# Half a phi moved ahead of the first x copy, the fourth numerators moved into the middle of out step 9, and two output copies swapped between engines: an attention and feed-forward kernel on one core

## The chip, the cores and the metric

The kernel runs on one core of a Trainium2 chip. The metric is the device time of one execution, in microseconds (us). The span of the profile runs from the program's first instruction to its last, and is some 2 us shorter than that time (324.5 against 326.26 us in the traced run of the kernel before). Names of engines: PE is the matmul engine, PEld its weight loads, DVE the vector engine, ACT the scalar engine, POOL the GpSimd engine, SP the engine whose queue issues most DMAs. L254 means line 254 of the kernel. Lines from 682 on carry a higher number in the changed kernel (L692 becomes L693), because a line was added before them.

## The reference

Batch 8, 8 heads, 576 tokens, head size 64; the result is a 4608 x 512 matrix.

```python
def phi(x, c, s):
    r = np.maximum(x, 0.0)
    return np.concatenate([r * c, r * s], axis=-1)   # cosine half, sine half
q_p, k_p = phi(q, cos_w, sin_w), phi(k, cos_w, sin_w)
kv  = einsum('bhsf,bhsd->bhfd', k_p, v);  z = k_p.sum over s
num = einsum('bhsf,bhfd->bhsd', q_p, kv)
den = einsum('bhsf,bhf->bhs', q_p, z)[..., None] + 1e-06
x   = (num / den), heads side by side: 4608 x 512
xn  = x / sqrt(mean(x * x) + 1e-6) * rms_g
out = (silu(xn @ w_gate) * (xn @ w_val)) @ w_out
```

## The kernel before

It works on one batch after another, and places every instruction by hand: each engine executes its own instructions in the order in which the source emits them. While PE runs the feed-forward part (FFN) of one batch, the other engines prepare the next. The change touches the opening (first x tiles of batch 0) and the end of block 0 (out steps, while batch 1 is prepared). "Numerators" are the matmuls of `nd_pe` (L414); an "x tile" is 128 tokens of x. Names that begin with ps are banks, the buffers that PE writes and that the other engines copy from. A "releaser" is the instruction whose end lets a waiting instruction start.

```python
def q_phi(eng, b, c, part):            # for batch 0 a q tile has two halves
    ...
        for i in range(2 if c < 4 else 1):
            j = 2 * c + i
            phi(eng, qp_tiles[(b, c)][:, 4*i : 4*i+4, o], raw[("q", 0)][...], f(5 + j))
...
# opening
    filler(7, psV[1][:, :])
    q_tr_pe(0, 2, psO[0][:, :])        # PE: transposes of q tile 2
    x_scale(0, 0)                      # DVE: x tile 0 scaled
    # x tile 0: PE transposes, half copied by ACT, half by DVE ("the first x copy")
    q_phi(A, 0, 3, 1)                  # ACT: sine half of q tile 3
    q_tr_evac(A, 0, 2, psO[0][:, :])   # ACT: copy of q tile 2's transposes
    x_norm(0, 1)                       # DVE: x tile 1 normalized
    q_phi(V, 0, 3, 0)                  # DVE: cosine half of q tile 3, two instructions
    open_ffn(0, (0, 1), 0, 128)        # PE: first FFN matmuls
    x_tr_pe(0, 1, psV[1][:, :])
    x_tr_evac(V, 0, 1, psV[1][:, :])
    q_tr_pe(0, 3, psO[1][:, :])        # PE: transposes of q tile 3
    nd_pe(0, 2, psA)                   # PE: numerators of x tile 2
    ...
# out steps of block 0: four banks, one per tile of 128 tokens
    for n in range(NNT - 2):
        ...
        if n == 9:
            x_norm(1, 1); tr1(0, psV[0][:, :])
        if n in nd_at:                 # numerators of batch 1, tile 3 at n == 9
            nd_pe(1, j, psA); nd_post(1, j, psA); x_sq(1, j)
        for j in range(4):
            out_mm(0, j, n, banks0[j])
    x_norm(1, 2)
    tr1(1, psV[1][:, :])               # PE transposes, ACT copies
    ...                                # n = 10, 11; copies of banks 2 (DVE) and 3 (ACT)
    gval_mm(1, 0, 0, (0, 256))         # PE: first matmuls of block 1
    tr1(2, psA[:, 0, :])
    out_store(V, 0, 1, banks0[1])
    x_norm(1, 3)
    out_store(A, 0, 0, banks0[0])
    gval_mm(1, 1, 1, (0, 256), ((psG, wg),))
    x_tr_pe(1, 3, psC[1][:, :]); x_tr_evac(V, 1, 3, psC[1][:, :])
```

`banks0` is psC0, psC1, psG0, psG1.

Of the kernel before, what the change touches and what calls it, by code (L numbers as in the profile page):

```python
# [26 lines left out]
def kernel(  # L27
# [39 lines left out]
    V, A, G = nc.vector, nc.scalar, nc.gpsimd  # L67
# [179 lines left out]
    def view4(t, j):  # L247
        return t[:, :, :].rearrange("p h (j d) -> p h j d", d=D)[:, :, j, :]

    def phi(eng, out_ap, in_ap, scale):  # L250
        if eng is nc.scalar:
            nc.scalar.activation(out=out_ap, in_=in_ap, func=AF.Relu, scale=scale)  # L252
        else:
            eng.tensor_scalar(  # L254
                out=out_ap, in0=in_ap, scalar1=scale, scalar2=0.0, op0=ALU.mult, op1=ALU.max
            )
# [24 lines left out]
            src = flat[:, 2048:2304].rearrange("p (i d) -> p i d", d=D)  # L281
        phi(eng, kp_of(b)[:, 8 * c : min(8 * c + 8, 36), o], src, f(c))

    def q_phi(eng, b, c, part):
        o = slice(0, D) if part == 0 else slice(D, F)
        f = cos_of if part == 0 else sin_of
        if (b, c) not in qp_tiles:
            qp_tiles[(b, c)] = four.tile(
                [P, H if c < 4 else 4, F], BF16, name="qp", tag="qp" if c < 4 else "qpt"
            )  # L290
        if b == 0:
            for i in range(2 if c < 4 else 1):
                j = 2 * c + i
                f = cos_of if part == 0 else sin_of
                phi(
                    eng, qp_tiles[(b, c)][:, 4 * i : 4 * i + 4, o],
                    raw[("q", 0)][:, :, j * D : (j + 1) * D], f(5 + j),
                )
            return
        src = view4(raw[("q", b)], c) if c < 4 else raw[("qt", b)][:, :, :]  # L300
        phi(eng, qp_tiles[(b, c)][:, :, o], src, f(c))
# [15 lines left out]
    def q_tr_pe(b, c, bank):  # L317
        t = qp_tiles[(b, c)]
        dst = bank.bitcast(BF16).rearrange("p (h s) -> p h s", s=P)
        for h in range(H if c < 4 else 4):  # L320
            nc.tensor.transpose(dst[:, h, :], t[:, h, :], ident[:, :])  # L321

    def q_tr_evac(eng, b, c, bank, heads=(0, 8)):
        h0, h1 = heads if c < 4 else (0, 4)
        if b == 0:
            src = bank.bitcast(BF16).rearrange("p (i h s) -> p h i s", i=2, h=H)
            copy(
                eng, q_dst(b, c)[:, h0:h1, :].rearrange("p h (i s) -> p h i s", i=2),
                src[:, h0:h1, :, :],
            )  # L330
            return
        dst = bank.bitcast(BF16).rearrange("p (h s) -> p h s", s=P)
        copy(eng, q_dst(b, c)[:, h0:h1, :], dst[:, h0:h1, :])

    def copy(eng, o, i):
        if eng is nc.scalar:
            nc.scalar.copy(out=o, in_=i)  # L337
        else:
            eng.tensor_copy(out=o, in_=i)  # L339
# [53 lines left out]
    def kvz_pe(b, pst):  # L393
        kvz_mm(b, [pst[:, c, :] for c in range(2)])
# [7 lines left out]
    def kvz_evac(eng, b, pst, c):  # L402
        kvz_copy(eng, b, c, pst[:, c, :])
# [94 lines left out]
    def x_scale(b, j):  # L498
        xn = four.tile([P, DM], BF16, name="xn", tag="xn")
        nc.vector.tensor_scalar(  # L500
            out=xn[:, :], in0=xg[:, :], scalar1=rs_of[(b, j)][:, :], scalar2=None, op0=ALU.mult
        )
        xn_of[(b, j)] = xn

    def x_norm(b, j):
        xn = four.tile([P, DM], BF16, name="xn", tag="xn")
        nc.vector.scalar_tensor_tensor(  # L507
            out=xn[:, :], in0=x_of[(b, j)][:, 0:DM], scalar=rs_of[(b, j)][:, :], in1=gb[:, :],
            op0=ALU.mult, op1=ALU.mult,
        )  # L510
        xn_of[(b, j)] = xn
# [16 lines left out]
    def x_tr_pe(b, j, bank, part=(0, NDT)):  # L528
        xn = xn_of[(b, j)]
        dst = bank.bitcast(BF16).rearrange("p (t s) -> p t s", s=P)  # L530
        for t in range(*part):
            nc.tensor.transpose(dst[:, t, :], xn[:, t * P : (t + 1) * P], ident[:, :])

    def x_tr_evac(eng, b, j, bank, part=(0, 4)):
        dst = bank.bitcast(BF16).rearrange("p (t s) -> p t s", s=P)
        copy(eng, x_dst(b, j)[:, part[0] : part[1], :], dst[:, part[0] : part[1], :])
# [5 lines left out]
    def gval_mm(blk, n, bank, cols=(0, TB), parts=((psG, wg), (psV, wv))):  # L542
        x = xnT[blk]
        for pst, w in parts:
            for t in range(NDT):
                nc.tensor.matmul(  # L546
                    pst[bank][:, cols[0] : cols[1]],
                    lhsT=w[:, t, n * P : (n + 1) * P],
                    rhs=x[:, t, cols[0] : cols[1]],
                    start=(t == 0), stop=(t == NDT - 1),  # L550
                )
# [13 lines left out]
    def out_mm(blk, j, n, bank):  # L565
        nc.tensor.matmul(  # L566
            bank, lhsT=hTs[blk][:, n, j * P : (j + 1) * P], rhs=wo[:, n, :],
            start=(n == 0), stop=(n == NNT - 1),
        )

    def out_store(eng, blk, j, bank):
        osb = four.tile([P, DM], FP32, name="osb", tag="osb")
        copy(eng, osb[:, :], bank)
        rows0 = out[0:S, :].rearrange("(p j) m -> j p m", j=NJ)
        if blk == 0:
            for i in range(2):
                nc.sync.dma_start(
                    out=rows0[2 * j + i, :, :], in_=osb[64 * i : 64 * i + 64, :]
                )
        elif blk < 8:  # L580
            rows = out[blk * S : blk * S + 512, :].rearrange("(p j) m -> p j m", j=4)
            nc.sync.dma_start(out=rows[:, j, :], in_=osb[:, :])
        else:
            for i in range(2):
                r0 = (2 * j + i) * S + 512
                nc.sync.dma_start(
                    out=rows0[8, :, :] if i + j == 0 else out[r0 : r0 + 64, :],
                    in_=osb[64 * i : 64 * i + 64, :],
                )
# [89 lines left out]
    filler(7, psV[1][:, :])  # L679
    q_tr_pe(0, 2, psO[0][:, :])  # L680
    x_scale(0, 0)

    def open_ffn(pair, steps, c0, c1, first=0, parts=(0, 1)):

        x = xnT[0]
        for i, n in enumerate(steps):
            for a in parts:
                w = (wg, wv)[a]
                bank = pairs[pair][a]
                lo = 256 * (first + i) + c0 % 256  # L690
                for t in range(NDT):
                    nc.tensor.matmul(  # L692
                        bank[:, lo : lo + c1 - c0],  # L693
                        lhsT=w[:, t, n * P : (n + 1) * P], rhs=x[:, t, c0:c1],
                        start=(t == 0), stop=(t == NDT - 1),
                    )
# [14 lines left out]
    for half, (eng, bank) in enumerate(((A, psG[1]), (V, psV[1]))):  # L711
        part = (2 * half, 2 * half + 2)
# [2 lines left out]
    q_phi(A, 0, 3, 1)  # L715
    q_tr_evac(A, 0, 2, psO[0][:, :])
    x_norm(0, 1)
    q_phi(V, 0, 3, 0)
    open_ffn(0, (0, 1), 0, 128)
    x_tr_pe(0, 1, psV[1][:, :])  # L720
    x_tr_evac(V, 0, 1, psV[1][:, :])
# [76 lines left out]
    for nb in range(2, B):  # L798
        b = nb - 1
# [30 lines left out]
        for j in range(4):  # L830
            n = nds[j]
# [12 lines left out]
    for nb in range(3, B):  # L844

        b = nb - 2
        for i, which in enumerate(("k", "v", "q")):
# [5 lines left out]
            for p in range(5):  # L853
                n = (0, None, 6)[i] + p if b == 1 else 5 * i + p
# [26 lines left out]
    banks0 = [psC[0][:, :], psC[1][:, :], psG[0][:, :], psG[1][:, :]]  # L881

    def tr1(j, bank):
        x_tr_pe(1, j, bank)
        x_tr_evac(A, 1, j, bank)
# [3 lines left out]
    for n in range(NNT - 2):  # L889
        if n == 3:  # L890
            kvz_pe(1, psA)
            kvz_evac(A, 1, psA, 0)
            kvz_evac(V, 1, psA, 1)
        if 1 <= n <= 4:
            c = n - 1
            q_tr_pe(1, c, qbank[c])
            q_tr_evac(V if c < 2 else A, 1, c, qbank[c])
        if n == 0:
            for c in (1, 2, 3):
                q_phi(V, 1, c, 0)  # L900
                q_phi(A, 1, c, 1)
        if n == 1:
            v_cast(A, 1, *LOW)
            v_cast(V, 1, *HIGH)
        if n == 3:
            d = load_q_tail(1)
            tc.add_manual_dep(d.ins, wo_dmas[1].ins.name, SYNC_DEP, reason="after wo")
            load_kv("k", 2)
            load_q(2)
            load_q_tail(2)  # L910
            load_kv("v", 2)
        if n == 7:
            x_norm(1, 0)
        if n == 9:
            x_norm(1, 1)
            tr1(0, psV[0][:, :])
        if n in nd_at:
            j = nd_at[n]
            nd_pe(1, j, psA)
            nd_post(1, j, psA)  # L920
            x_sq(1, j)
        for j in range(4):
            out_mm(0, j, n, banks0[j])
    x_norm(1, 2)
    tr1(1, psV[1][:, :])
# [5 lines left out]
    for j in (0, 1):  # L931
        for n in (NNT - 2, NNT - 1):
            out_mm(0, j, n, banks0[j])
    gval_mm(1, 0, 0, (0, 256))
    tr1(2, psA[:, 0, :])
    out_store(V, 0, 1, banks0[1])
    x_norm(1, 3)
    out_store(A, 0, 0, banks0[0])
    gval_mm(1, 1, 1, (0, 256), ((psG, wg),))
    x_tr_pe(1, 3, psC[1][:, :])  # L940
    x_tr_evac(V, 1, 3, psC[1][:, :])
# [72 lines left out]
```

## Time and profile before

| | before |
|---|---|
| time, median of 6 runs | 326.46 us (326.31 to 326.73) |
| span of the profile | 324.5 us |
| PE busy | 316.2 us, 97% |
| DVE, ACT busy | 57%, 54% |

The page cuts the span into 40 slices of 8.1 us and gives each engine's busy share in tenths:

```profile
PE   8999999999999999999999999999999999999995
DVE  6875768787656765578267745772577133203410
ACT  6974865965665556645555466455644333223321
```

PE is full from the second slice on. DVE and ACT have room on average, but one of them or both are at 7 to 9 in slices 2, 3, 7 and 8, where the change acts. There an engine with a mean of 57% can hold PE up for a few tenths of a microsecond, and the change aims at such places. The prediction below shows their lines.

```profile
54.91 0.56 ACT L337 COPY xnT<-psV 128x512 bf16<-128x512 bf16 x1
55.58 0.60 PE L546 MATMUL psG<-xnT,wg 128*128 128x256 bf16 x4
```

The first is ACT's copy of x tile 1's transposes. It ends at 55.48, and PE's psG matmul at 55.58 reads what it wrote. That matmul starts 0.22 us after the one in front of it, as those before it do, so in this kernel the copy doesn't hold it up yet.

### The profile page before, as it was taken

The page shows a single profiled execution, that of the slowest core. Times are in us where ns is not written, and L with a number is a line of the kernel's source. Part 1 is how long each engine was busy: PE and PEld are TensorE (multiplying, and loading weights), DVE is VectorE, ACT ScalarE, POOL GpSimd, SP SyncE. Part 2 cuts the span into 40 slices and gives each one's busy share as a digit, 9 for nine tenths or more (in the row PEclk, how much of TensorE's full clock was granted, in tenths as well). Part 3 has the DMA queues.
Part 4 walks back from the last instruction along what each step waited for, and adds up shares of the span by engine and source line. Part 5 has one row for each costly group of instructions (what it writes and reads, how often), then busy time and mean ns, then how long its engine had stood idle before and what let it go on. Part 6 is the DMA issues. An engine that isn't in the chain of part 4 may idle for free.

```text
span 324.5 us, 6131 instructions
## 1 busy us (share of the span) xinstructions
PE 316.2 (97%) x2249; PEld 162.4 (50%) x2284; DVE 184.3 (57%) x398; ACT 173.8 (54%) x351; POOL 39.3 (12%) x85
## 2 busy tenths in 40 slices
PE   8999999999999999999999999999999999999995
PEld 3588465555445444554454445444544444444443
DVE  6875768787656765578267745772577133203410
ACT  6974865965665556645555466455644333223321
POOL 4660202001111110012001120120011000000000
PEclk9999999999999999999999999999999999999999
DMA  7999999898799775977597679856611400020014
GB/s 271 281 196 253 309 205 339 243 165 189 164 248 273 190 205 153 237 163 195 165 214 206 155 219 210 194 158 215 128 40 33 131 32 0 25 106 0 1 33 100
DMA packets 89377, 53.90 MB, mean 166 GB/s; under 512 B 56321, under 2 KB 81921, under 8 KB 89346
## 3 DMA queue, kind: packets, MB, share of 16 engines
q1 hardware_dynamic: 82304, 48.65, 57.4%
q0 software_dynamic: 6880, 4.72, 10.0%
q8 instruction: 18, 0.29, 0.4%
q10 hardware_dynamic: 162, 0.13, 0.2%
q14 instruction: 13, 0.11, 0.1%
HBM read 37.75 MB, written 9.44 MB: 145 GB/s over the span
## 4 chain that ended last, share of the span: by engine, by line
PE 93%; DVE 2%; ACT 2%; issue 1%; POOL 0%; DVEq 0%
PE psC L566 26%; PE psV L546 26%; PE psG L546 26%; PE psA L414 2%; PE psO L593 2%; PE psA L370 2%; PE psG L566 2%; PE psO L692 1%; PE psG L692 1%; PE psV L692 1%; PE psV L321 1%; ACT kpm L252 1%; PE psA L386 1%; ACT sg L555 0%; PE psA L422 0%
## 5 line engine op out<-in xcount | busy, mean ns | idle before, releaser
L561 DVE TENSOR_TENSOR hT<-psV,sg 128x512 bf16<-128x512 f32 x102 | 70.3, 689 | 96.0 <-PE psV L546 71.2
L555 ACT ACTIVATE sg<-psG 128x512 f32<-128x512 f32 x102 | 60.6, 594 | 64.5 <-PE psG L546 63.2
L546 PE MATMUL psV<-xnT,wv 128*128 128x512 bf16 (+1 forms) x365 | 92.1, 375 | 0.4
L546 PE MATMUL psG<-xnT,wg 128*128 128x512 bf16 (+1 forms) x352 | 90.9, 375 | 0.7
L566 PE MATMUL psC<-wo,hT 128*128 128x512 bf16 x382 | 88.2, 380 | 0.7
L546 PEld LDWEIGHTS <-wv 128*128 128x128 bf16 x416 | 40.6, 98 | 47.4
L566 PEld LDWEIGHTS <-hT 128*128 128x128 bf16 x420 | 40.2, 98 | 46.7
L546 PEld LDWEIGHTS <-wg 128*128 128x128 bf16 x416 | 38.5, 98 | 40.8 <-DVE xnT L339 0.4
L485 POOL TENSOR_TENSOR rs<-ms,mhalf 128x1 f32<-128x1 f32 x36 | 19.8, 549 | 187.6 <-ACT scr L480 187.6
L337 ACT COPY osb<-psC 128x512 f32<-128x512 f32 (+1 forms) x33 | 19.1, 579 | 43.1 <-PE psC L566 42.4
L507 DVE SCALAR_TENSOR_TENSOR xn<-xt,rs,gb 128x512 bf16<-128x512 f32 x35 | 26.5, 757 | 16.4 <-POOL rs L485 16.3
L480 ACT ACTIVATE scr<-xt 128x513 bf16<-128x513 f32 x36 | 22.9, 635 | 23.7 <-DVE xt L469 23.6
L252 ACT ACTIVATE kpm<-rk,tab 128x256 bf16<-128x256 f32 (+2 forms) x58 | 28.2, 545 | 1.5 <-DMA rk<-in_k_dram 1.5
L469 DVE TENSOR_TENSOR xt<-psA,rec 128x512 f32<-128x512 f32 x35 | 24.2, 691 | 1.2
L252 ACT ACTIVATE qp<-rq,tab 128x512 bf16<-128x512 f32 (+1 forms) x37 | 23.7, 661 | 0.0
L254 DVE TENSOR_SCALAR kpm<-rk,tab 128x128 bf16<-128x128 f32 (+2 forms) x64 | 20.5, 377 | 2.1 <-DMA rk<-in_k_dram 2.1
L254 DVE TENSOR_SCALAR qp<-rq,tab 128x512 bf16<-128x512 f32 (+1 forms) x37 | 16.0, 452 | 0.0
L414 PEld LDWEIGHTS <-qpT 128*128 128x128 bf16 x248 | 11.7, 98 | 6.7 <-issue 0.3
L414 PE MATMUL psA<-kvzs,qpT 128*128 128x65 bf16 x248 | 12.8, 194 | 0.3
L546 PE MATMUL psG<-xnt_tail,wg 128*128 128x512 bf16 x48 | 12.3, 379 | 0.1
L546 PE MATMUL psV<-xnt_tail,wv 128*128 128x512 bf16 x47 | 12.1, 379 | 0.0
L339 DVE CAST vvm<-rv 128x1024 bf16<-128x1024 f32 (+4 forms) x16 | 10.4, 674 | 0.0
(99 smaller groups left out, 183.8 us busy)
## 6 DMA issues: line engine op xcount, KB each, us to landing
out_dram<-osb SPq DMA_DIRECT2D x28, 256.0 KB, 2.5
rk<-in_k_dram SPq DMA_DIRECT2D x20, 256.0 KB, 3.2
rq<-in_q_dram SPq DMA_DIRECT2D x20, 256.0 KB, 3.1
rv<-in_v_dram SPq DMA_DIRECT2D x16, 256.0 KB, 3.2
rq<-in_q_dram SPq DMA_DIRECT2D x2, 1024.0 KB, 9.2
out_dram<-osb SPq DMA_DIRECT2D x14, 128.0 KB, 3.2
rv<-in_v_dram SPq DMA_DIRECT2D x3, 576.0 KB, 8.4
wo<-in_moe_w_out_dram POOLq DMA_DIRECT2D x4, 384.0 KB, 7.1
```

The source lines that it names most:

```text
L252: nc.scalar.activation(out=out_ap, in_=in_ap, func=AF.Relu, scale=scale)
L254: eng.tensor_scalar(out=out_ap, in0=in_ap, scalar1=scale, scalar2=0.0, op0=ALU.mult, op1=ALU.max)
L337: nc.scalar.copy(out=o, in_=i)
L414: nc.tensor.matmul(o[:, g, i, :], lhsT=qpT[(b, 0)][:, h, j * P : (j + 1) * P], rhs=kvz_of(b, h), start=True, stop=True,)
L469: nc.vector.tensor_tensor(out=xt[:, 0:DM].rearrange("p (b h d) -> p b h d", b=2, d=D), in0=o[:, :, :, 0:D], in1=rec[:, :, :].unsqueeze(3). ...
L480: nc.scalar.activation(out=scr[:, :], in_=xt[:, 0 : DM + 1], func=AF.Square, scale=1.0 / math.sqrt(DM), accum_out=ms[:, :],)
L485: nc.gpsimd.tensor_tensor(out=rs[:, :], in0=ms[:, :], in1=mhalf[:, :], op=ALU.pow)
L507: nc.vector.scalar_tensor_tensor(out=xn[:, :], in0=x_of[(b, j)][:, 0:DM], scalar=rs_of[(b, j)][:, :], in1=gb[:, :], op0=ALU.mult, op1=ALU. ...
L546: nc.tensor.matmul(pst[bank][:, cols[0] : cols[1]], lhsT=w[:, t, n * P : (n + 1) * P], rhs=x[:, t, cols[0] : cols[1]], start=(t == 0), sto ...
L555: nc.scalar.activation(out=sg[:, :], in_=psG[bank][:, :], func=AF.Silu)
L561: nc.vector.tensor_tensor(out=hTs[blk][:, n, :], in0=psV[bank][:, :], in1=sg[:, :], op=ALU.mult)
L566: nc.tensor.matmul(bank, lhsT=hTs[blk][:, n, j * P : (j + 1) * P], rhs=wo[:, n, :], start=(n == 0), stop=(n == NNT - 1),)
```

## The change

Its intent: let DVE do half of the late phi in an idle spell, give PE two output matmuls to do where it waited for a bank, and give DVE's copy of psC1 to ACT, so that the last normalization comes sooner.

```diff
-    def q_phi(eng, b, c, part):
+    def q_phi(eng, b, c, part, subs=(0, 1)):
...
-            for i in range(2 if c < 4 else 1):
+            for i in subs if c < 4 else (0,):
...
     x_scale(0, 0)
+    q_phi(V, 0, 3, 0, (0,))
...
-    q_phi(V, 0, 3, 0)
+    q_phi(V, 0, 3, 0, (1,))
...
             tr1(0, psV[0][:, :])
+        for j in range(2) if n == 9 else ():
+            out_mm(0, j, n, banks0[j])
         if n in nd_at:
...
-        for j in range(4):
+        for j in range(2 if n == 9 else 0, 4):
             out_mm(0, j, n, banks0[j])
...
+    out_store(A, 0, 1, banks0[1])
     tr1(2, psA[:, 0, :])
-    out_store(V, 0, 1, banks0[1])
     x_norm(1, 3)
-    out_store(A, 0, 0, banks0[0])
+    out_store(V, 0, 0, banks0[0])
```

## The prediction

> **What bounds the kernel now.** I read the page first: shares of busy time, then the chain that ended last.
>
> ```profile
> PE 316.2 (97%) x2249; PEld 162.4 (50%) x2284; DVE 184.3 (57%) x398; ACT 173.8 (54%) x351; POOL 39.3 (12%) x85
> PE 93%; DVE 2%; ACT 2%; issue 1%; POOL 0%; DVEq 0%
> ```
>
> PE is busy for 97% of the span, and the chain of work that ended last runs through it for 93%. The change removes no PE instruction, so only holes in PE's stream can be won, and those hide in the 324.5 - 316.2 = 8.3 us outside its busy time. So I went to the timeline at the places that the diff touches, about 15 to 20 us and 51 to 58 us (columns: start, us, engine, line, operation, count, idle time before).
>
> First place, the transposes of q tile 3 (L321) around the first x tiles:
>
> ```profile
> 15.97 0.49 DVE L500 TENSOR_SCALAR xn<-sg,rs 128x512 bf16<-128x512 f32 x1
> 16.95 0.29 DVE L339 COPY xnT<-psV 128x256 bf16<-128x256 bf16 x1 [0.49 <-PE psV L532]
> 17.36 0.75 DVE L507 SCALAR_TENSOR_TENSOR xn<-xt,rs,gb 128x512 bf16<-128x512 f32 x1
> 17.91 1.00 ACT L337 COPY qpT<-psO 128x1024 bf16<-128x1024 bf16 x1
> 18.03 0.89 DVE L254 TENSOR_SCALAR qp<-rq,tab 128x256 bf16<-128x256 f32 x2
> 18.49 0.24 PEld L321 LDWEIGHTS <-qp 128*128 128x128 bf16 x4
> 19.07 0.38 PE L321 MATMUL psO<-ident,qp 128*128 128x128 bf16 x4 [0.16 <-DVE qp L254]
> 19.29 0.41 PE L414 MATMUL psA<-kvzs,qpT 128*128 128x65 bf16 x8
> ```
>
> DVE sits idle for 0.49 us before the first x copy at 16.95. Later, two phi instructions (L254) occupy it from 18.03 to 18.92, and the last four q transposes begin only at 19.07, right behind them. A finer window shows the two phis as 0.34 us and 0.63 us, the long one beginning at 18.29.
>
> Second place, out step 9:
>
> ```profile
> 52.39 0.74 DVE L507 SCALAR_TENSOR_TENSOR xn<-xt,rs,gb 128x512 bf16<-128x512 f32 x1
> 52.52 0.40 PE L414 MATMUL psA<-kvzs,qpT 128*128 128x65 bf16 x8
> 53.05 0.16 DVE L465 TENSOR_SCALAR rec<-psA 128x8 f32<-128x8 f32 x1
> 54.09 0.74 DVE L507 SCALAR_TENSOR_TENSOR xn<-xt,rs,gb 128x512 bf16<-128x512 f32 x1
> 54.74 0.68 DVE L339 COPY osb<-psG 128x512 f32<-128x512 f32 x1
> 55.48 0.41 PEld L546 LDWEIGHTS <-wg 128*128 128x128 bf16 x4 [0.24 <-DVE osb L339]
> ```
>
> PE has issued the four transposes of x tile 0 from 52.00 on (four at 0.055, so to 52.22) and then waits to 52.52 for psA, which DVE reads to 52.47: a hole of 0.30 us. But DVE works back to back from 51.34 to 55.42, and PE's weight load at 55.48 waits for that very DVE copy of psG.
>
> Third place, the block's two last copies:
>
> ```profile
> 55.78 0.69 DVE L339 COPY osb<-psC 128x512 f32<-128x512 f32 x1 [0.35 <-PE psC L566]
> 56.38 0.74 DVE L507 SCALAR_TENSOR_TENSOR xn<-xt,rs,gb 128x512 bf16<-128x512 f32 x1
> 57.18 0.23 PEld L532 LDWEIGHTS <-xn 128*128 128x128 bf16 x4 [0.19 <-DVE xn L507]
> 57.62 0.42 DVE L339 COPY xnT<-psC 128x512 bf16<-128x512 bf16 x1 [0.49 <-PE psC L532]
> 58.10 0.33 PEld L546 LDWEIGHTS <-wg 128*128 128x128 bf16 x4 [0.36 <-DVE xnT L339]
> ```
>
> The normalization of x tile 3 stands behind an output copy; PE waits for it at 57.18, and again at 58.10 for the copy of its transpose.
>
> **What the Trainium skill says.** (1) "VectorE: DVE Perf Modes", section "Mode 2×_2P": a single-source instruction on SBUF operands can stream one tensor through both read ports, two results per cycle even in fp32. The trace agrees: phi takes 0.34 us for 256 elements and 0.47 for 512, so 0.13 us per 256 more. (2) "SBUF — State Buffer", section "SBUF: two separate sides": such an instruction and GpSimd exclude each other by a lock on a shared port pair. It fits that the 0.63 us phi lies beside weight DMA issues of POOL (18.05 to 18.80); that this is the cause the trace doesn't prove. (3) "Perfetto Trace Analysis", section "Tensor Engine Instruction (MATMUL, LD_WEIGHTS)": matmul ends are modelled, so I count holes from start to start.
>
> **The change part by part.** The order of instructions built from both kernels shows the same work everywhere, only moved.
>
> *Part 1, half a phi ahead of the first x copy.* The scaling of x at 15.97 lets DVE go on at about 16.4. A phi of 0.34 ends at about 16.75, before the copy can start at 16.95 (POOL is idle from 15.94 to 16.77, so I expect no stretching). The normalization at 17.36 waits for POOL's result (16.77 + 0.55), so it stays. The remaining phi takes the place of the quick one, 18.03 to 18.37. PE: x transposes from 18.17 to 18.39; first q half at once (it needs no late phi now), 18.39 instead of 18.52; second half at 18.61 instead of 19.07; all eight issued by 18.83. That would win 19.29 - 18.83 = 0.46. But the numerators (L414) need the copy of q tile 2 by ACT, 17.91 + 1.00 = 18.91, and with a handover of 0.06 (57.12 to 57.18 in the third place) they begin at about 18.98. Part 1 wins 19.29 - 18.98 = **0.31 us**. The copy of x tile 1 moves to about 18.62 to 19.02, in time.
>
> Does a later wait eat it? The timeline has PE nearly dense from 19.3 to 43.9; its waits there go to instructions which PE itself releases. Landings, from the DMA view (issue plus time to landing) against first use: third wv slice 13.93 + 8.5 = 22.4 against 23.56; fifth wg slice 18.78 + 11.9 = 30.7 against about 35; q of batch 1 30.84 + 7.3 = 38.1 against 40.2; v of batch 1 40.9 against 42.6; second wo slice 43.6 against 45.6. The smallest slack is 1.1 us, so 0.31 passes through.
>
> *Part 2, two output matmuls between the transposes and the fourth numerators.* They take 2 x 0.216 = 0.43 us and fill the hole of 0.30, so numerators begin at 52.65 instead of 52.52 and PE arrives 0.30 earlier at the end of the out steps. But DVE's post-processing of these numerators, at 53.05 before, now starts at 52.65 + 0.41 + 0.04 = 53.10. DVE's row (normalization, copy of psG) slides by 0.05 and ends at about 55.47; PE can load at 55.53 and its matmul begins at about 55.55 instead of 55.58. Part 2 alone wins **0.03 us**: the hole moves from 52.2 to before 55.5.
>
> *Part 3, the swap.* ACT takes the psC copy after its own at 55.38 (ends about 56.0), so to about 56.6. DVE goes from the psG copy to normalization 3, which must wait for POOL's factor (55.09 + 0.55 = 55.64, plus 0.05), and ends at about 56.5 instead of 57.12. PE then reaches its transposes without a wait: 55.55 + 0.43 + 0.44 + 0.22 + 0.43 = 57.07 instead of 57.19; psC is free by then. DVE is free for the copy of the transpose, so the hole before 58.10 keeps its length and moves with it, to 57.98. Parts 2 and 3 together win **0.12 us**. Up to 67.7 the chain is ACT and DVE work released by PE at 59.6, with k, q and v of batch 2 long landed (v at 49.72 + 9.9 = 59.6, used at 65.2); from there on it is PE again.
>
> Sum: 0.31 + 0.12 = 0.43 us, so 326.41 - 0.43 = **325.98 us**.
>
> **Rivals.** (a) *The hole of step 9 is won whole.* It would add some 0.27, so 325.7. For: 0.30 us of PE idleness does vanish. Against: DVE's unbroken row to 55.42 and the wait at 55.48. (b) *Part 1 costs where it should win:* the early phi is stretched like the 0.63 us one, ends at 17.03 and delays the x copy by 0.08, and the first FFN matmul with it. Its second pair of weights has about 0.1 us of slack, so even then little is lost; if POOL stretched the second phi as well, transposes would end near 19.1 and part 1 would win 0.2. Time 326.1. (c) *The opening's gain dies at a transfer:* 326.3. The landings speak against it. (d) *ACT becomes the bound in part 3:* with two output copies in a row it would free psC late. I count 56.6 against a need at 57.07; a miss of 0.3 would leave 326.2.
>
> **Range and chances.** The central sum is 0.43; rivals lie between 325.7 and 326.3, and runs of the kernel before differ by 0.25 among themselves. So 325.6 to 326.45. Over 2% would be 6.5 us, fifteen times the sum: 0.005 on either side.
>
> **What would show it.** Right: a 0.34 us phi inside DVE's idle time before 16.95; q transposes without a wait inside; numerators at about 18.98 released by ACT's copy, not by DVE; no hole near 52.2 (less 0.31 for the shift), but one of about 0.25 before the psG matmul at 55.2; no wait for normalization before the last transposes; span about 324.05. Wrong: the first FFN matmul later than 17.3; the shift at 30 us smaller than 0.25; a psG matmul 0.3 us earlier than I have it; a wait for ACT before the last transposes.

## The result, and the profile after

| | before | changed |
|---|---|---|
| time, median of 6 runs | 326.46 us (326.31 to 326.73) | 326.05 us (325.86 to 326.24) |
| span of the profile | 324.5 us | 324.1 us |

The ratio is 0.9987, with a 95% interval of 0.9974 to 0.9999. Ratios here are the mean time of one kernel's fast runs over that of the other's of the same rounds, so not quite the ratio of the medians quoted. The page of the changed kernel:

```profile
PE 317.8 (98%) x2284; PEld 162.2 (50%) x2284; DVE 184.7 (57%) x398; ACT 173.9 (54%) x351; POOL 39.1 (12%) x85
PE 90%; DVE 5%; ACT 2%; DMA 1%; issue 1%; DVEq 0%; ACTq 0%
```

PE's busy time seems to have gone up by 1.6 us. It has not: the trace before holds 2249 matmuls and this one 2284, for the same number of weight loads. Thirty-five records were missing before. So the 8.3 us outside PE's busy time, from which the prediction sets out, are too many: 6.3 us by the complete trace. This is why the rest of this document goes by starts, not by busy time.

**First place**, timeline of the changed kernel:

```profile
15.90 0.49 DVE L500 TENSOR_SCALAR xn<-sg,rs 128x512 bf16<-128x512 f32 x1
16.30 0.35 DVE L254 TENSOR_SCALAR qp<-rq,tab 128x256 bf16<-128x256 f32 x1
16.88 0.29 DVE L339 COPY xnT<-psV 128x256 bf16<-128x256 bf16 x1 [0.23 <-PE psV L532]
17.84 1.00 ACT L337 COPY qpT<-psO 128x1024 bf16<-128x1024 bf16 x1
17.95 0.35 DVE L254 TENSOR_SCALAR qp<-rq,tab 128x256 bf16<-128x256 f32 x1
18.33 0.61 PE L321 MATMUL psO<-ident,qp 128*128 128x128 bf16 x8
18.90 0.42 PE L414 MATMUL psA<-kvzs,qpT 128*128 128x65 bf16 x8
```

The early phi lies in what was DVE's idle time. The late one takes 0.35 us, the eight q transposes run in one piece, and the numerators come right after the end of ACT's copy (17.84 + 1.00 = 18.84).

**Second and third place:**

```profile
52.28 0.41 PE L414 MATMUL psA<-kvzs,qpT 128*128 128x65 bf16 x8
52.72 0.17 DVE L465 TENSOR_SCALAR rec<-psA 128x8 f32<-128x8 f32 x1
54.43 0.68 DVE L339 COPY osb<-psG 128x512 f32<-128x512 f32 x1
54.60 0.57 ACT L337 COPY xnT<-psV 128x512 bf16<-128x512 bf16 x1
55.16 0.36 PEld L546 LDWEIGHTS <-wg 128*128 128x128 bf16 x4 [0.59 <-DVE osb L339]
55.21 0.60 PE L546 MATMUL psG<-xnT,wg 128*128 128x256 bf16 x4
55.35 0.75 DVE L507 SCALAR_TENSOR_TENSOR xn<-xt,rs,gb 128x512 bf16<-128x512 f32 x1 [0.24 <-POOL rs L485]
56.74 0.39 PE L532 MATMUL psC<-ident,xn 128*128 128x128 bf16 x4
57.24 0.42 DVE L339 COPY xnT<-psC 128x512 bf16<-128x512 bf16 x1 [0.53 <-PE psC L532]
57.72 0.33 PEld L546 LDWEIGHTS <-wg 128*128 128x128 bf16 x4 [0.43 <-DVE xnT L339]
```

The hole before the numerators is gone, but PEld now idles 0.59 us before the psG load at 55.16, where it idled 0.24 before. The psG matmul waits for two copies that end almost together: DVE's at 55.11 (54.43 + 0.68) and ACT's at 55.17. The normalization no longer stands behind an output copy, and PE reaches the transposes at 56.74 without a wait. Yet the last weight load waits longer than before, 0.43 against 0.36.

**How shifts are measured from here on.** The opening's DMAs land a little differently in each run: DVE's first work on the loaded k starts between 4.35 and 4.81 us. In the fourteen traces the first FFN weight load behind the copies of x tile 0 starts between 17.19 and 17.64 us. In all of them it starts 1.29 us after DVE's scaling of x tile 0, which stands ahead of every change; so the early phi between the two doesn't delay it, and it can serve as the zero. PE executes the same list of weight loads in nearly the same order in all kernels (2284; e10_best splits some and has 2288), and none of their records is missing. So I take the start of the same weight load in two traces, after subtracting the difference at that first FFN load. A negative shift is earlier.

| shift of the changed kernel against before | us |
|---|---|
| numerators of x tile 2 (19 us) to out step 8 (50 us) | -0.31 |
| transposes of x tile 3 (57 us) | -0.38 |
| second tile pair of block 1 (59 us) | -0.31 |
| last weight load of the kernel | -0.32 |

So the changed kernel gains 0.31 us in the opening and nothing after it. Against the 0.40 us by which its span is shorter, 0.07 us is this trace's earlier first FFN load, which the change doesn't move.

### The profile page after: what moved, and what is told of

Same layout as the page of the kernel before. It is cut to its first block, busy times and chain, and to the rows that moved or that the text cites. A ratio compares the mean times of both kernels' runs of the same rounds, so it can differ in the third digit from the quotient of the medians.

```text
span 324.1 us, 6166 instructions
## 1 busy us (share of the span) xinstructions
PE 317.8 (98%) x2284; PEld 162.2 (50%) x2284; DVE 184.7 (57%) x398; ACT 173.9 (54%) x351; POOL 39.1 (12%) x85
## 4 chain that ended last, share of the span: by engine, by line
PE 90%; DVE 5%; ACT 2%; DMA 1%; issue 1%; DVEq 0%; ACTq 0%
PE psG L546 26%; PE psC L566 26%; PE psV L546 26%; PE psA L414 2%; PE psA L370 2%; DVE kpm L254 1%; PE psG L693 1%; PE psV L693 1%; DMA rk<-in_k_dram 1%; PE psO L693 1%; PE psG L566 1%; DVE vvm L339 1%; ACT kpm L252 1%; DVE qp L254 1%; PE psA L386 1%
## 5 line engine op out<-in xcount | busy, mean ns | idle before, releaser
L546 PE MATMUL psG<-xnT,wg 128*128 128x512 bf16 (+1 forms) x368 | 92.8, 374 | 0.3 <-DVE xnT L339 0.2
L566 PE MATMUL psC<-wo,hT 128*128 128x512 bf16 x396 | 89.4, 379 | 0.0
```

The lines of the kernel that those rows point to most:

```text
L546: nc.tensor.matmul(pst[bank][:, cols[0] : cols[1]], lhsT=w[:, t, n * P : (n + 1) * P], rhs=x[:, t, cols[0] : cols[1]], start=(t == 0), sto ...
L566: nc.tensor.matmul(bank, lhsT=hTs[blk][:, n, j * P : (j + 1) * P], rhs=wo[:, n, :], start=(n == 0), stop=(n == NNT - 1),)
```

## The experiments

Twelve kernels ran, on three chips; each gave the reference's result. "Shift" is against the kernel before, as above. Times are medians of the fast runs. e7_act_early, e8_dve_early and e12_both_phis_early ran once, so their state is unknown; they are used for their traces alone. e11_pool_quiet is told below.

| kernel | shift at 59 us | shift at the end | time, us | before, same chip |
|---|---|---|---|---|
| changed | -0.31 | -0.32 | 326.05 | 326.46 |
| e1_part1 | -0.31 | -0.31 | 326.31 | 326.40 |
| e2_step9 | -0.07 | -0.07 | 326.94 | 326.40 |
| e3_swap | -0.02 | +0.02 | 326.42 | 326.40 |
| e4_step9_swap | 0.00 | +0.40 | 326.44 | 326.40 |
| e5_no_swap | -0.38 | -0.39 | 326.12 | 326.37 |
| e6_one_wait | -0.38 | -0.39 | 326.18 | 326.37 |
| e7_act_early | -0.35 | -0.36 | 326.00 | 326.37 |
| e8_dve_early | -0.31 | -0.32 | 326.15 | 326.37 |
| e9_both | -0.62 | -0.63 | 325.81 | 326.37 |
| e10_best | -0.92 (63 us) | -0.57 | 325.52 | 326.37 |
| e12_both_phis_early | -0.31 | -0.32 | 326.03 | 326.37 |

Runs of one kernel differ by 0.3 to 1.1 us, so most of the times can't tell these kernels apart. The shifts can: where two kernels have the same instructions in a stretch, they agree within about 0.02 us, apart from one spot at 97 us (e4_step9_swap, e10_best).

### One part at a time

My theory after reading the traces was that part 1 is the whole gain. The rival was the prediction's sum, in which all three parts give.

**e1_part1**: the kernel before with part 1 alone.

```diff
     x_scale(0, 0)
+    q_phi(V, 0, 3, 0, (0,))
...
-    q_phi(V, 0, 3, 0)
+    q_phi(V, 0, 3, 0, (1,))
```

> Only the half phi of q tile 3 is moved ahead of the first x copy; the rest is the kernel before. Theory (part 1 is the whole gain, parts 2 and 3 give nothing): the numerators of x tile 2 start 0.31 us earlier than before, counted from the first FFN matmul at 17.2 (before: 19.29 - 17.26 = 2.03 us after it, here about 1.72), and that 0.31 is still there at 60 us and at the end; total about 326.1. Rival (all three parts give, as predicted: 0.31 + 0.12): the same 0.31 here, and the changed kernel faster than this one by 0.12.

The shift is -0.31 from the numerators to the end, as in the changed kernel. The theory holds for the shift. The time of 326.31 us is above the expected 326.1: in the traced run, which is also the median, the first FFN load came at 17.63 us, 0.37 later than in the trace before, which hides the gain. By the clock the ratio is 0.9995 (0.9983 to 1.0008), which can't show 0.1%.

**e2_step9**: the kernel before with the two output matmuls moved.

```diff
+        for j in range(2) if n == 9 else ():
+            out_mm(0, j, n, banks0[j])
         if n in nd_at:
```

> Only the two output matmuls of step 9 ahead of the fourth numerators. Theory: the hole of 0.30 us before those numerators is gone, but the psG matmul at 55.6 is not earlier (within 0.03), because ACT's copy of x tile 1's transpose and DVE's copy of psG both end only then; a hole of about 0.3 stands there instead; at 60 us the kernel is 0.00 to 0.03 later than before. As predicted: 0.03 earlier. Rival (the hole is won whole): 0.27 to 0.30 earlier. Total 326.4, 326.4 and 326.1.

The psG matmul starts 0.02 us later than before, as the theory has it: the hole moved and was not won. The shift at 59 us is nonetheless -0.07, which neither theory nor prediction expected. The trace shows why. The last output matmul starts 0.29 us earlier (37.82 us after the first FFN load instead of 38.10), so DVE begins its copy of psC1 straight after that of psG, and the normalization behind it ends at 39.58 instead of 39.87. PE no longer waits for it. Step 9 alone had freed the normalization.

This kernel's four runs took 326.29 (the traced one), 326.73, 327.15 and 327.36 us. The ratio is 1.0021 (1.0006 to 1.0036), slower by 0.2%, against its own trace. The three longer runs left no trace, so their cause stays open. A candidate stands under e4_step9_swap.

**e3_swap**: the kernel before with the swap alone.

```diff
+    out_store(A, 0, 1, banks0[1])
     tr1(2, psA[:, 0, :])
-    out_store(V, 0, 1, banks0[1])
     x_norm(1, 3)
-    out_store(A, 0, 0, banks0[0])
+    out_store(V, 0, 0, banks0[0])
```

> Only the swap of the two copies. Theory: PE's wait of 0.09 before the transposes of x tile 3 goes, but DVE's copy of them has two releasers now and starts 0.06 later after the last transpose (0.32 instead of 0.26), so the psG matmul at 58.1 is 0.02 to 0.03 earlier. As predicted (no such cost): 0.09 earlier. Total 326.4 either way.

-0.02 at 59 us, as the theory says. PE's wait before the transposes is gone (-0.08 there), and most of it is lost at the copy behind them.

**e4_step9_swap**: both, without part 1.

> Parts 2 and 3 without part 1. Theory: 0.00 to 0.03 us at 60 us against the kernel before. As predicted: 0.12 earlier. If the parts were coupled (part 1's shift spoils them in the changed kernel), 0.12 shows here and not there.

0.00 at 59 us. The parts aren't coupled with part 1; the swap takes back the 0.07 of step 9. The +0.40 at the end comes at one spot. These lines are from this kernel's timeline:

```profile
97.01 0.69 DVE L339 CAST vvm<-rv 128x1024 bf16<-128x1024 f32 x1
97.06 1.34 POOL L339 CAST vvt<-rv 64x256 bf16<-64x256 f32 x2 [6.67 <-DMA rv<-in_v_dram]
98.00 0.19 PE L370 MATMUL psA<-vvt,kpm 128*128 128x65 bf16 x1 [0.25 <-POOL vvt L339]
```

The last piece of v of batch 3 landed as DVE began a copy of its own. POOL's first copy took 0.88 us, where it takes 0.39 in the trace of the changed kernel, in which it began at 96.12, well ahead of DVE's. PE waited for it. In the trace before, POOL's pair began at 96.92, 0.09 ahead of DVE's copy; there POOL's first copy took 0.43, and DVE's 0.89 instead of 0.69. So a landing 0.15 us later, counted from the first FFN load, cost 0.4 us here. The edit doesn't touch this load, so I take it for chance; one trace can't say how often it happens.

### The swap's cost

**e5_no_swap**: the changed kernel without its swap.

> The changed kernel without the swap: parts 1 and 2 alone. Theory (the swap gives nothing beside step 9 and costs 0.06 us through the second releaser of DVE's copy): from 60 us on, counted from the first FFN matmul, 0.06 to 0.07 us earlier than the changed kernel, 0.38 earlier than before. As predicted (the swap is what frees the normalization): 0.09 later than the changed kernel. Total 326.0 by the theory, 326.15 as predicted.

-0.38: the changed kernel without the swap is 0.07 us earlier than with it. By the clock the two can't be told apart (ratios to before 0.9995 and 0.9987, with intervals of about 0.0013 on either side).

Where do the 0.07 go? In the built program, DVE's copy of x tile 3's transposes waits for PE alone before the change, and for PE and ACT after it, because ACT now reads psC1 too; the traces record the same semaphores, one before and two after. The chain of waits of the changed kernel (start, us, what; DVEq is DVE's sequencer) shows the second wait as an instruction of its own:

```profile
57.17 0.02 DVEq L339
57.19 0.04 issue
57.24 0.44 DVE xnT L339
```

**e6_one_wait**: the swap stays, but those transposes go to a bank that DVE read last. Tile 2's transposes take psC1 instead, so ACT's copies of banks 1 and 3 change places.

```diff
     out_store(V, 0, 2, banks0[2])
-    out_store(A, 0, 3, banks0[3])
...
     out_store(A, 0, 1, banks0[1])
-    tr1(2, psA[:, 0, :])
+    out_store(A, 0, 3, banks0[3])
+    tr1(2, psC[1][:, :])
...
-    x_tr_pe(1, 3, psC[1][:, :])
-    x_tr_evac(V, 1, 3, psC[1][:, :])
+    x_tr_pe(1, 3, psA[:, 1, :])
+    x_tr_evac(V, 1, 3, psA[:, 1, :])
```

> The changed kernel, its swap kept, with the transposes of x tile 3 in the second bank of psA, which DVE read last, and those of tile 2 in psC1, so that DVE's copy of tile 3's transposes waits for PE alone. Theory (two releasers cost 0.06): that copy starts 0.26 us after the last transpose instead of 0.32, and the kernel is 0.06 earlier from 60 us on than the changed kernel. Rival (the delay is in the bank or in DVE's own row): 0.32 stays and nothing is won.

The copy starts 0.257 us after the start of the last transpose. In the changed kernel it is 0.324, in the kernel before, from the same bank psC1, 0.258. So the bank doesn't matter. The shift is -0.38. In the seven traces with a second releaser the delay is 0.324 or 0.325 us and the extra instruction is recorded; in the seven others it is 0.256 to 0.265 and there is none. The second releaser costs 0.07 us, and this is shown.

### What holds the psG matmul at 55 us

**e7_act_early**: ACT copies x tile 1 before it squares tile 3.

```diff
             nd_post(1, j, psA)
-            x_sq(1, j)
+            if n != 9:
+                x_sq(1, j)
...
     tr1(1, psV[1][:, :])
+    x_sq(1, 3)
```

> The changed kernel with ACT copying x tile 1's transposes before it squares tile 3, so ACT's releaser of the psG matmul at 55.2 comes 1.1 us sooner. Theory (ACT's copy and DVE's copy of psG end 0.05 apart and both hold that matmul): it starts only 0.03 to 0.05 earlier, held by DVE. If ACT alone held it: 0.31 earlier, at PE's own pace.

The psG matmul starts 0.05 us earlier than in the changed kernel: DVE's copy still holds it.

**e8_dve_early**: DVE copies psG before it normalizes tile 2.

```diff
-    x_norm(1, 2)
     tr1(1, psV[1][:, :])
...
     out_store(V, 0, 2, banks0[2])
+    x_norm(1, 2)
```

> The changed kernel with DVE copying psG before it normalizes x tile 2, so DVE's releaser comes 0.65 us sooner. Theory: the psG matmul at 55.2 doesn't move (0.00), held by ACT. If DVE alone held it, as predicted: 0.31 earlier.

It doesn't move (0.00): ACT's copy holds it.

**e9_both**: both edits.

> Both orders of the last two runs together. Theory: the psG matmul goes to PE's own pace, 0.30 us earlier than in the changed kernel, and the hole that step 9 pushed there is won at last; the double releaser stays, so 0.25 to 0.30 earlier from 60 us on; total 325.75. If a third wait stands behind the two: less than 0.1.

```profile
54.06 0.69 DVE L339 COPY osb<-psG 128x512 f32<-128x512 f32 x1
54.30 1.03 PE L566 MATMUL psC<-wo,hT 128*128 128x512 bf16 x4
55.16 0.60 PE L546 MATMUL psG<-xnT,wg 128*128 128x256 bf16 x4
```

Counted from the first FFN load, the psG matmul starts 0.31 us earlier than in the changed kernel, at PE's own pace (0.22 us after the matmul in front of it), and all of it reaches the end (-0.63). Each releaser alone gives 0.05 us or nothing, and both together give the whole hole: of two waits that end 0.05 us apart, a view that names one releaser shows only one. The ratio is 0.9982 (0.9968 to 0.9995).

### A faster version

**e10_best**: e9_both with e6's banks (tile 2 in psC1, tile 3 in psA), the next gate matmul split so that a quarter fills the hole before the wait for tile 3, and v of batch 3 loaded last piece first.

```diff
+    gval_mm(1, 0, 0, (256, 384), ((psG, wg),))
+    gval_mm(1, 0, 0, (384, 512), ((psG, wg),))
     for n in range(2):
-        gval_mm(1, n, n, (256, 512))
+        gval_mm(1, n, n, (256, 512), ((psG, wg), (psV, wv))[1 - n :])
...
+                at(b, 13, "post", load_last, "v", nb)
                 at(b, 13, "post", load_heads, "v", nb, 0, 4)
                 at(b, 14, "post", load_heads, "v", nb, 4, 8)
-                at(b, 14, "post", load_last, "v", nb)
```

> The two orders, the one-releaser banks, a quarter of the next gate matmul drawn into the hole before the wait for tile 3, and the last piece of v of batch 3 loaded first. Theory: 0.6 us earlier than the changed kernel from 60 us on, about 325.45; POOL's copy of that v piece at 96 us starts over 1 us sooner, so its lottery ends and the runs lie closer together. If the v piece or another transfer binds once the kernel is that much earlier: some of the 0.6 is lost at 97 us, and 325.7.

At 63 us the shift is -0.92, so 0.61 ahead of the changed kernel, as expected. The cure for the v piece did not work. POOL's copy starts at 91.75 instead of 96.12, but now the heads that were loaded after it land last: DVE's copy of them starts at 97.07, idle for 0.60 before that, and PE loses 0.35 us to it. The traced run was the slowest of five, 325.98; the others took 325.40 to 325.74. The ratio is 0.9976 (0.9964 to 0.9989). This is the fastest kernel, 0.85 us below the kernel before by the medians.

### Where part 1's gain comes from

**e11_pool_quiet**: the kernel before, with POOL's last weight loads issued later. It is slow by design in the later stages (330.31 us); only the opening counts.

```diff
     x_sq(0, 1)
-    gval_slice(768, 1152)
-    gval_slice(1152, 1536)
...
     x_sq(0, 2)
+    gval_slice(768, 1152)
+    gval_slice(1152, 1536)
     wo_load(0)
```

> The kernel before with POOL's last four weight loads issued later, so that POOL issues nothing between 17.3 and 19 us (later stages then wait for weights: only the stretch to 20 us counts). Theory (POOL's issue stretches the second phi): both phis take 0.34 us, the last q transposes start 0.3 earlier than before, and the numerators are then held by ACT's copy: they start 0.30 earlier without any move. Rival (the second phi is long by itself): 0.63 again and nothing moves.

From its timeline:

```profile
17.39 0.38 PE L690 MATMUL psG<-xnT,wg 128*128 128x128 bf16 x4 [0.35 <-ACT xnT L337]
18.16 0.61 DVE L254 TENSOR_SCALAR qp<-rq,tab 128x256 bf16<-128x256 f32 x2
19.14 0.41 PE L414 MATMUL psA<-kvzs,qpT 128*128 128x65 bf16 x8
```

In the kernel before, POOL's issue and the second phi stood like this:

```profile
18.05 0.75 POOL L236 DMA_DIRECT2D wv<-in_moe_w_val_dram  x1
18.29 0.63 DVE L254 TENSOR_SCALAR qp<-rq,tab 128x256 bf16<-128x256 f32 x1
```

Both phis take 0.35 us now, and the numerators start 19.14 - 17.39 = 1.75 us after the first FFN matmul, against 2.03 before and 1.71 in the changed kernel. So nearly all of what the move won (0.28 of 0.31) is what POOL's weight issues had cost the second phi.

**e12_both_phis_early**: the changed kernel with the whole phi ahead of the first x copy.

> The changed kernel with both phis ahead of the first x copy. Theory: two phis end about 0.05 after the time at which the copy could start, so the copy starts up to 0.1 later, the first FFN matmul loses less than 0.05 because its first two weights need the other half; the numerators, held by ACT's copy of q tile 2, start where they do in the changed kernel (1.71 after the first FFN matmul), within 0.05. Rival (numerators held by phi): 0.1 or more earlier.

The numerators start 1.71 us after the first FFN load, as in the changed kernel, so phi doesn't hold them any more; ACT's copy does. DVE's copy of x starts on time. The cost shows elsewhere: POOL's factor for x tile 1 takes 0.62 us instead of 0.55, and x tile 1's transposes come 0.06 later, but the wait for ACT's copy hides it.

## Why the prediction was right or wrong

The measured 326.05 us lies 0.07 from the predicted 325.98 and inside its range. The mechanism of part 1 was right, those of parts 2 and 3 were not, and that the total came so near is in part luck: runs of one kernel differ by 0.3 us and more.

- **Part 1, predicted 0.31: shown, 0.31** (e1_part1, and the changed kernel from 19 us to 50 us). Each step is as worked out: the early phi inside DVE's idle time, no delay to the first FFN matmul (1.29 us after the scaling of x, as before), numerators held by ACT's copy and not by DVE (e12_both_phis_early). The remark that POOL's issues might have stretched the second phi was only argued there; e11_pool_quiet shows it.
- **No later wait eats it: shown.** The 0.31 is still there at the last weight load. One landing was misread: 40.9 us for v of batch 1 is worked out with the median of two loads, the later of which lands at 41.43, so its slack is 1.2 and not 1.7 us. The conclusion stands.
- **Part 2, predicted 0.03.** The claim that "the hole moves from 52.2 to before 55.5" is right. The step that fails is that the psG matmul waits for DVE's copy only and begins at 55.55. DVE's row slid by 0.07 instead of 0.05 (e2_step9). ACT's copy of x tile 1 ends 0.05 us later than DVE's and holds it too, so the psG matmul lost 0.02 instead of gaining 0.03 (e7, e8 and e9 show the two releasers). On the other hand, step 9 alone gave 0.07 us downstream: earlier outputs let DVE reach the normalization sooner. The prediction gave this effect to the swap.
- **Part 3, with part 2 predicted 0.12: measured 0.00** (e4_step9_swap). The failing step is that "the hole before 58.10 keeps its length and moves with it". It grew by 0.07 (the wait behind PE's own pace went from 0.25 to 0.32 us), because DVE's copy of the transposes got a second releaser (e6_one_wait). Without the swap the 0.07 of step 9 stays (e5_no_swap). The built program had shown the added wait before any run; I read only its order of instructions there.
- **Rivals.** (a) The hole is not won whole by the change; e9_both shows what it takes. (b), (c) and (d) did not come: no stretching of the early phi, no transfer that took the opening's gain, no wait for ACT before the last transposes.
- **The total.** The sum that the traces show is 0.31 and not 0.43. The medians differ by 0.41, but the interval of the ratio (0.9974 to 0.9999) allows 0.03 to 0.85 us.

## What to carry to other kernels

When an engine waits for two others, look for the end of each, not for the one that the profile names: removing one of two tied waits won 0.05 us or nothing here, and the hole that was filled ahead of them only moved. Moving work to another engine adds a releaser to whatever touches the same bank next, and that wait can have a price (0.07 us here); compare the waits of the built programs as well as their order. When the effects are tenths of a microsecond and runs differ by more, compare the starts of one engine's instructions in two traces, counted from a point that the change is shown not to move.

## What the Trainium skill lacked or had wrong

- "Perfetto Trace Analysis", section "Identifying Dependency Chains", says that an instruction waiting on several engines may get extra EventSemaphore instructions ahead of it, but not what that costs. Here a second releaser, recorded as such an instruction, put 0.07 us ahead of a DVE copy (0.324 against 0.257 us from the start of the last transpose).
- "SBUF — State Buffer", section "SBUF: two separate sides", says that of a DVE two-port instruction and a GpSimd one, the one that starts first blocks the other fully. The traces agree: a DVE phi that began behind a weight issue of POOL took 0.63 instead of 0.35 us (e11_pool_quiet), and a phi that began 0.02 us ahead of an issue was not stretched (18.03 before, 17.95 after). What the page lacks is the size of this hold: the stretched phi ended 0.12 us after the recorded end of the issue (18.92 against 18.80) in all four traces in which this phi is stretched.
- No page that I read has a size for a collision between copies of these shapes: POOL's copy of 64 x 256 took 0.88 instead of 0.39 us when it began 0.06 us after one of DVE (e4_step9_swap), and DVE's took 0.89 instead of 0.69 us when POOL's began 0.09 us ahead of it (the kernel before). That the lock is its cause is in line with that page, and no run here separates it.
